# Split constant loads, early row ends, more fillers and a new list of steps in a state-space, MLP and expert kernel

## The chip, the cores and the metric

The kernel runs on one core of a Trainium2 chip, in one launch. The metric is the device time of that launch in microseconds (us). Five engines take part, each with its own stream of instructions: PE (matmuls, with its weight loads listed apart as PEld), DVE (vector), ACT (scalar), POOL (GpSimd) and SP (which here mostly issues DMAs). An engine runs its stream in order; where one needs what another makes, it waits on a semaphore.

## The reference, cut to what matters

```python
# stage 1: state-space recurrence; batch 4, heads 8, sequence 768, head size 32, state 16
log_a = np.log(np.clip(a, 1e-06, 1.0))
for c in range(768 // 32):
    cum = np.cumsum(la, axis=-1)                       # inside the chunk
    M = np.einsum('bhin,bhjn->bhij', Cc, Bc) * np.exp(cum_i - cum_j) * causal
    y = M @ xc + (Cc @ state) * np.exp(cum)
    state = np.exp(sum(la)) * state + sum_j Bc_j xc_j * np.exp(cum[-1] - cum_j)
x = y.transpose(0, 2, 1, 3).reshape(3072, 256)
# stage 2: dense MLP, d_ff 2048
x = np.maximum(x @ w_in, 0) ** 2 @ w_out
# stage 3: 8 experts, one for each token, d_ff 1024
logits = normalised(x) @ normalised(expert_emb).T / tau
e = argmax(logits); gate = softmax(logits)[e]
out = gate * (np.maximum(x @ w1[e], 0) @ w2[e])
```

## The kernel before, in words

The 3072 tokens are 24 tiles of 128 partitions, in 6 groups of 4. Stage 1 works a tile at a time: a few tables are made from the logarithms of the decays `a` by matmuls with constant masks (`tables` L1051, `tables2` L1065 and L1067, `tables3` L1084 and L1090; the masks are the constant `c1`, 128x903 in f32, of which columns 0 to 511 serve `tables`, columns 512 to 774 the two others, and 8 rows of the last 128 columns line L1090). Then come the scores (L811), their decay (DVE L829), the mask (POOL L837), the output (L922) and the state. The squares of each tile (ACT L949) decide its scale (DVE L968).

Stage 2 runs 16 blocks of d_ff for each group as "units" (first products L1250, relu and square on ACT and DVE, second products L1269); they fill PE from about 37 us to 343 us, beside stage 1 of later tiles. When a group is ready, `route` picks each token's expert and POOL scatters the rows to a table in DRAM, ordered by expert (L1461, an indirect DMA for each tile).

Stage 3 is 31 "jobs" of up to 128 rows of one expert: 13 from a first table made after group 4, 15 from a second, and 3 under an If. A job is: `job_load` (SP, transposed read of the rows, L1607), first products (L1634, 12 matmuls), relu in two parts (ACT L1714, DVE L1716), a transpose by DMA (SP L1645), second products (L1662 and L1664, 8 pairs), `job_result` (ACT L1677, then DVE L1680, both scaled by the gate), `job_send` (POOL L1687, indirect DMA to the output). The gate and the destination of a row stand in four 16-bit columns at its end, 512 to 515. `job_ends` reads these (a DMA on ACT's queue, L1703) and multiplies the gate by a factor on DVE (L1705). The numbers of rows and experts come into registers by `load_regs` (L1553), on PE once for each table.

The order of all this is written out by hand: each piece of work is a Python generator that yields its engine and an assumed duration (`yield "T", 2.6` is PE for 2.6 us), and `weave()` (L390) takes the next step of the generator that the table `ORDER` names. What it emits, the engines run in that order. The durations decide nothing of the order where the table names each step; they are used in one more place, `keep_warm` (L474): where the plan leaves PE idle in the beginning, it puts filler matmuls (L477, 128x176 on zeros, results unused), so many for each planned idle microsecond (4.799 up to 6 us, 4.8 later). The filler's zeros are written by DVE first (L1898).

SP's loads go through `load` (L483, issue at L485). The first ones are a part of C (`ct`), the decays, `c1`, the expert embedding, `b_t`, `tau` and two pieces of w_in, then `x`, `bc` (B and C by token) and `c2`.

Of the kernel before, what the change touches and what calls it, by code (L numbers as in the profile page):

```python
# [9 lines left out]
F32 = mybir.dt.float32  # L10
# [6 lines left out]
ALU = mybir.AluOpType  # L17
# [7 lines left out]
H = 8  # L25
# [27 lines left out]
           q1=343.921, q2=43.866, q3=196.988, slack=0.043, warm=4.8, cold=4.799, u0=0.5, d0=97.094, m0=24.87,  # L53
           m1=1.248, u1=17.747, du=77.015, t0=111.371, t1=50.866, t2=54.217, t3=156.529, t4=129.206, t5=39.718,
           oz=3.191, oa=57.9, ob=23.917, ou=158.402, oc=-54.916, og=172.157, ol=101.876, ev=-1.454, fin=10.03,
           rt=-25.056, fin5=77.015, rt5=83.245, e0=75.531, e1=19633888, e2=0.024, e3=2113488, wi=0.043, pi=48831578,
           pi1=-87.702, wo=61.294, po=0.263, po1=0.042, l1=69.922, emb=129.297, con=-28.03, fj=63.956, fe=92.693,
           oj=48519990, pd=95.005, oe=83.994, lj=-6.608, l0=199.952, v0=0.75, v1=0.25, v2=1, ps=176, wq=-6.586,
           c0=71.046, c1=-111.128, uh=43.261, mh=52.693, sn=14)

ORDER = (
# [1912 lines left out]
```

## Time and profile before

| | us |
|---|---|
| median of 3 runs | 510.75 (509.02 to 510.91) |
| the profiled execution's own time | 510.88 |
| its span in the trace | 509.2 |
| PE busy | 486.0 (95%) |
| ACT, DVE, POOL busy | 350.9, 321.2, 158.0 |

The span is that of the trace; 1.7 us of the execution's own time lie around it. PE busy 95% of the span means that only 23 us are left in which PE does nothing, 7.5 of them behind its last matmul. The share says nothing on where these are, nor which of the busy time is fillers. The clock granted to PE is 0.988 of the full one on average: it was full except between about 9 and 16 us, where it was half. The chain that ended last goes through PE for 70% of the span, DVE and DMA for 8% each and ACT for 6%.

### The profile page before, as it was taken

How to read it: one execution, taken by the hardware profiler on the slowest of the kernel's cores; microseconds unless marked ns; L12 is line 12 of the kernel's file. 1: busy time of each engine (PE TensorE's matmuls, PEld its weight loads, DVE VectorE, ACT ScalarE, POOL GpSimd, SP SyncE). 2: the span in 40 equal slices, each digit the busy share in tenths (PEclk: the TensorE clock that was granted, in tenths of full speed). 3: DMA queues.
4: the chain of work that ended last, by engine and by line, in shares of the span. 5: the costliest groups of instructions: out<-in, count | busy, mean ns of one | idle time of the engine just before them, and what ended most of it. 6: DMA issues, size and time to landing. Idle time of an engine off the chain costs nothing.

```text
span 509.2 us, 11796 instructions
## 1 busy us (share of the span) xinstructions
PE 486.0 (95%) x4057; PEld 316.8 (62%) x4057; DVE 321.2 (63%) x917; ACT 350.9 (69%) x735; POOL 158.0 (31%) x186
## 2 busy tenths in 40 slices
PE   8889999999999999999999999999998989999994
PEld 7656467766776776676667676665554445455552
DVE  4788966788868988868656856855764223234331
ACT  3889896698989889999999999875232123233321
POOL 0667655556574332500210120110030403031222
PEclk8899999999999999999999999999999999999997
DMA  8980003355153651335405231024898659797872
GB/s 280 404 313 2 2 11 106 105 157 164 41 201 54 156 136 44 115 115 187 176 33 121 98 127 31 23 66 81 137 197 158 165 117 177 124 182 142 142 127 58
DMA packets 112204, 64.59 MB, mean 127 GB/s; under 512 B 101253, under 2 KB 105615, under 8 KB 109072
## 3 DMA queue, kind: packets, MB, share of 16 engines
q1 hardware_dynamic: 105616, 57.38, 45.7%
q0 software_dynamic: 2496, 6.40, 3.7%
q10 hardware_dynamic: 4032, 0.03, 0.6%
q8 instruction: 36, 0.59, 0.5%
q14 instruction: 24, 0.20, 0.1%
HBM read 32.58 MB, written 8.13 MB: 80 GB/s over the span
## 4 chain that ended last, share of the span: by engine, by line
PE 70%; DVE 8%; DMA 8%; ACT 6%; issue 5%; ACTq 0%; POOL 0%; POOLq 0%; SPq 0%; DVEq 0%
PE bank L1250 20%; PE bank L1269 17%; PE bank L1634 10%; DMA out<-work 6%; PE bank L1662 5%; PE bank L811 3%; PE bank L922 2%; PE bank L1664 2%; PE bank L1159 2%; DMA work<-xs 1%; PE bank L917 1%; PE bank L1198 1%; ACT wexp L693 1%; PE bank L989 1%; DVE wexp L829 1%
## 5 line engine op out<-in xcount | busy, mean ns | idle before, releaser
L1250 PE MATMUL bank<-work 128*128 128x256 f16 x1152 | 136.5, 273 | 1.3 <-DVE work L1290 1.3
L1250 PEld LDWEIGHTS <-work 128*128 128x128 f16 x1152 | 111.4, 98 | 24.3 <-issue 2.0
L1269 PE MATMUL bank<-work 128*128 128x512 f16 x480 | 113.3, 379 | 0.0
L1662 PE MATMUL bank<-wexp,work 128*128 x224 | 74.0, 379 | 4.9 <-DVE work L1680 2.5
L1634 PE MATMUL bank<-wexp,work 128*128 x336 | 76.5, 379 | 1.1 <-DVE work L1716 1.1
L1269 PEld LDWEIGHTS <-work 128*128 128x128 f16 x480 | 46.3, 99 | 43.9
L1714 ACT ACTIVATE work<-bank 128x512 f16<-128x512 f32 x56 | 32.0, 597 | 54.4 <-PE bank L1634 36.7
L1461 POOL DMA_INDIRECT xs<-work x24 | 27.4, 1141 | 114.2 <-ACT work L1274 73.7
L1687 POOL DMA_INDIRECT out<-work x28 | 27.3, 975 | 112.6 <-DVE work L1680 70.8
L1664 PE MATMUL bank<-wexp,work 128*128 x224 | 61.0, 273 | 0.0
L1290 DVE TENSOR_TENSOR work<-work 128x512 f16<-128x512 f32 x68 | 46.2, 687 | 20.3 <-ACT work L1286 19.9
L1634 PEld LDWEIGHTS <-work 128*128 128x128 f16 x336 | 32.6, 98 | 37.9 <-issue 1.5
L837 POOL TENSOR_SCALAR_AFFINE_SELECT wexp<-wexp 128x512 f32<-128x512 f32 x48 | 36.4, 758 | 62.5 <-DVE wexp L829 45.4
L1716 DVE SCALAR_TENSOR_TENSOR work<-bank,work 128x512 f16<-128x512 f32 x56 | 36.8, 684 | 27.4 <-ACT work L1714 26.6
L1274 ACT ACTIVATE work<-bank 128x512 f32<-128x512 f32 x80 | 47.1, 591 | 10.0 <-PE bank L1269 7.4
L1286 ACT CAST work<-work 128x512 f16<-128x512 f32 x80 | 48.7, 616 | 3.1 <-DVE work L1282 2.0
L1677 ACT ACTIVATE work<-bank,work 128x256 f32<-128x256 f32 x28 | 13.2, 474 | 51.8 <-PE bank L1664 21.0
L829 DVE TENSOR_TENSOR wexp<-bank,wexp 128x256 f32<-128x256 f32 x96 | 37.9, 416 | 6.5 <-PE bank L811 4.5
L1279 ACT ACTIVATE work<-work 128x512 f32<-128x512 f32 x64 | 40.2, 630 | 0.4
L1662 PEld LDWEIGHTS <-work 128*128 128x128 f16 x224 | 21.9, 98 | 26.6 <-issue 0.5
L1680 DVE SCALAR_TENSOR_TENSOR work<-bank,work 128x256 f32<-128x256 f32 x28 | 13.5, 481 | 26.0 <-ACT work L1677 25.7
L1664 PEld LDWEIGHTS <-work 128*128 128x128 f16 x224 | 21.9, 98 | 9.5 <-issue 5.2
(246 smaller groups left out, 743.4 us busy)
## 6 DMA issues: line engine op xcount, KB each, us to landing
wexp<-in_w SPq DMA_DIRECT2D x8, 1024.0 KB
work<-in_w SPq DMA_DIRECT2D x8, 1024.0 KB
wexp<-in_w_in SPq DMA_DIRECT2D x4, 1024.0 KB
wexp<-in_w_out SPq DMA_DIRECT2D x4, 1024.0 KB
wexp<-in_x SPq DMA_DIRECT2D x6, 512.0 KB
wexp<-in_ct SPq DMA_DIRECT2D x6, 256.0 KB
wexp<-in_bc SPq DMA_DIRECT2D x6, 256.0 KB
xs<-work SPq DMA_DIRECT2D x9, 132.0 KB
```

The lines of the kernel that those rows point to most:

```text
L829: V.tensor_tensor(mv, ps.rearrange("p (a b) -> p a b", b=32), eg[:, t, n * q:n * q + n].rearrange("p h q -> p (h q)").unsqueeze(2) .to_bro ...
L837: G.affine_select(out=mm, in_=mm, pattern=[[0, 4], [1, P]], compare_op=ALU.is_ge, fill=0.0, base=0, channel_multiplier=-1)
L1250: T.matmul(po, gg[:, s], wout[:, wi, f], start=(f == 0 and n == 0 and k % 2 == 0), stop=(f == NF - 1 and n == 2), skip_group_check=True)
L1269: T.matmul(p, win[:, wi, kk, f * P:(f + 1) * P], x[:, xi * 2 + kk], start=(n == 0), stop=(n == 5))
L1274: S.activation(r, p, AF.Relu, scale=XK)
L1279: S.activation(r, r, AF.Square)
L1286: S.copy(gh, r)
L1290: V.tensor_tensor(gl, r, gh, ALU.subtract)
L1634: T.matmul(p, xj[i][:, xi * 2 + kk], W[:, bass.ds(e, 1), c0:c0 + 512].rearrange("p a b -> p (a b)"), start=(n == 0), stop=(n == 5))
L1662: T.matmul(po, r[:, f], W[:, bass.ds(e, 1), c0:c0 + 512].rearrange("p a b -> p (a b)"), start=(f == 0), stop=False, skip_group_check=True)
L1664: T.matmul(po[:, 0:DM], r[:, 8 + f], W[:, bass.ds(e, 1), c0:c0 + 256].rearrange("p a b -> p (a b)"), start=False, stop=(f == 7), skip_grou ...
L1716: V.scalar_tensor_tensor(out=rh[:, 1, s], in0=p, scalar=0.0, in1=rh[:, 0, s], op0=ALU.max, op1=ALU.subtract)
```

## The change

All arithmetic stays, apart from the number of fillers (55 before, 75 now). The changed parts are:

- `c1` is loaded in three pieces, first columns 512 to 774, then 0 to 511, then the 8 rows of 128, each with a mark of its own that the tables wait for.
- The decays are loaded by a DMA on ACT's queue, the first thing in ACT's stream, ahead of its table load; before, SP issued it second.
- The filler's zeros are written by POOL instead of DVE.
- `job_ends` starts with the job's row load instead of behind the transpose of its relu, and has 13 buffers for its factor instead of 5, so that it needs no result of the job two before.
- The last job (27) does its eight 512-wide second products first and the eight 256-wide ones behind them.
- Many assumed durations are new, the fillers are 6.5 (up to 7 us) and 11 (later) for each planned idle microsecond, and the table `ORDER` is new from end to end.

```diff
-           q1=343.921, q2=43.866, q3=196.988, slack=0.043, warm=4.8, cold=4.799, u0=0.5, d0=97.094, m0=24.87,
+           q1=343.921, q2=43.866, q3=196.988, slack=0.043, warm=11, cold=6.5, u0=0.5, d0=97.094, m0=24.87, m1=1.248,
...
-    "3.1 0 1 23 3.0 23.0 7 8 3.2 3.3 24 15 15 5 23 19 21 17 5 16 23 45 23 23 21 19 5 22 45 17 23 23 23 5 21 55 22 "
+    "0 1 5.1 3 5.0 2 4 6.0 5.3 5.2 9 10 6.1 26 17 17 7 24 24 18 47 7 7 47 19 23 19 7 23 57 69 20 21 22 23 21 8 57 "
...
-    ffj = [A.take([1], F32) for _ in range(5)]
+    fft = A.take([16], F32)
+    ffj = [fft[:, i:i + 1] for i in range(13)]
...
-                keep_warm((s - free[eng]) * (DUE["warm"] if s > 6 else DUE["cold"]))
+                keep_warm((s - (free[eng] or 0.5)) * (DUE["warm"] if s > 7 else DUE["cold"]))
             free[eng] = s + cost
-            th[2] = s + cost + LAT
+            th[2] = s + cost + LAT + sum(what for what in th[3][2:] if type(what) is float)
...
@@ job_load
         reads_rows(Q.dma_start_transpose(out=xj[i].bitcast(I16), in_=row_at(r, 0, 512)), table)
         yield "mark", ("xj", j)
+        yield "spawn", job_ends(j, table)
...
@@ job
         Q.dma_start_transpose(out=rT[j % 4], in_=flat(rh))
         yield "mark", ("rT", j)
-        yield "spawn", job_ends(j, table)
         yield "due", job_due(j)
...
-        yield "T", 2.6, (pbank(j),)
+        last = j == JU - 1
+        yield "T", 1.73 if last else 2.6, (pbank(j),)
         for f in range(8):
...
-            T.matmul(po[:, 0:DM], r[:, 8 + f], W[:, bass.ds(e, 1), c0:c0 + 256].rearrange("p a b -> p (a b)"),
-                     start=False, stop=(f == 7), skip_group_check=True)
+            if not last:
+                low_half(j, f)
+        if last:
+            yield "mark", ("m2h", j)
+            yield "T", 0.95, (pbank(j),)
+            for f in range(8):
+                low_half(j, f)
...
@@ job_ends
-        yield "need", ("rows_s", table)
-        yield "need", ("out", before(j, 2))
-        yield "need", ("sent", j - NXJ)
-        yield "S", 0.45
+        for key in (("rows_s", table), ("out", j - NXJ), ("sent", j - NXJ)):
+            yield "need", key
+        yield "S", 0.4, 4.2
         reads_rows(S.dma_start(fi[i].bitcast(I16), xs[bass.ds(rows_s[j], P), 512:516]), table)
         yield "V", 0.1, "L"
-        V.tensor_tensor(ffj[j % 5], fi[i][:, 0:2].bitcast(F32), fjob[:, j:j + 1], ALU.mult)
+        V.tensor_tensor(ffj[i], fi[i][:, 0:2].bitcast(F32), fjob[:, j:j + 1], ALU.mult)
...
-    th = [(0, load(flat(la), a_tok, 0.27, ("ald", 0))), (DUE["lc"], load(c1_s, c1, 2.3, ("c1", 0))),
+    k0 = 4 * P, 6 * P + 7
+    th = [(-1e3, log_inputs()), (DUE["lc"], load(c1_s[:, k0[0]:k0[1]], c1[:, k0[0]:k0[1]], 0.5, ("c1", 0))),
+          (DUE["lc"], load(rr_s, c1[0:H, k0[1]:], 0.05, ("c1", 2))), (DUE["lc"], load(c1_s[:, 0:k0[0]], c1[:, 0:k0[0]], 0.8, ("c1", 1))),
...
-        V.memset(idle_s, 0.0)
+        G.memset(idle_s, 0.0)
+        S.dma_start(flat(la), a_tok)
         S.preload_act_table_set("natural_log_exp_and_others")
-        free["S"] = 1.3
+        free.update(S=1.8, V=1.0, G=0.6, Q=0.8)
```

SP's loads now come in the order `c1` (128x263), `ct`, `c1` (128x512), `b_t`, `c1` (8x128), `c2`, `bc` twice, `x`, w_in twice, `ct`, w_in twice, the embedding and so on; `tau` is the 23rd load instead of the 6th. The embedding's preparation (L1099, some ten small instructions on DVE) stands among tiles further on.

The first place is PE's stream at the start. Before, 26 fillers stand ahead (the last is the first row here), then the tables (L1065, L1084, L1051), a sum over C (L755) and the first tile's scores (L811):

```order
L477 MATMUL bank_67<-wexp 128x176
L1065 MATMUL bank_69<-wexp 128x32
L1084 MATMUL bank_64<-wexp 8x5 x4
L1051 MATMUL bank_69<-wexp 128x32 x4
L755 MATMUL bank_63<-wexp 128x128 x4
L1084 MATMUL bank_64<-wexp 8x5 x20
L1090 MATMUL bank_64<-wexp 128x20
L811 MATMUL bank_67<-wexp 128x128
L811 MATMUL bank_68<-wexp 128x128
```

Now 22 fillers stand ahead (L478 is the old L477, L1089 the old L1084, L756 the old L755, L1056 the old L1051):

```order
L478 MATMUL bank_67<-wexp 128x176
L1089 MATMUL bank_64<-wexp 8x5 x20
L756 MATMUL bank_63<-wexp 128x128 x4
L1056 MATMUL bank_69<-wexp 128x32 x4
L1089 MATMUL bank_64<-wexp 8x5 x4
L478 LDWEIGHTS wexp
L478 MATMUL bank_67<-wexp 128x176
L478 LDWEIGHTS wexp
```

The table with the 128x263 piece comes first, the 128x32 matmul of L1065 has gone behind the first tile's scores (as L1070), and five fillers (two of them shown) stand ahead of the scores. The seven fillers that stood between the first and the second tile's scores are gone from there; seven now stand behind the second tile's scores and the first tile's output.

The second place is ACT's stream in the jobs. Before, loads of row ends (L1703) stand one by one among the relus (L1714) and the results (L1677):

```order
L1714 ACTIVATE work<-bank_68 128x512
L1714 ACTIVATE work<-bank_64 128x512
L1703 ISA
L1703 DMA work<-xs 128x4
L1714 ACTIVATE work<-bank_63 128x512
L1714 ACTIVATE work<-bank_67 128x512
L1703 ISA
L1703 DMA work<-xs 128x4
L1677 ACTIVATE work<-bank_65,work 128x256
L1703 ISA
L1703 DMA work<-xs 128x4
L1714 ACTIVATE work<-bank_68 128x512
```

Now (L1720 is the old L1703, L1731 the old L1714, L1695 the old L1677):

```order
L1731 ACTIVATE work<-bank_67 128x512
L1731 ACTIVATE work<-bank_68 128x512
L1720 ISA
L1720 DMA work<-xs 128x4
L1720 ISA
L1720 DMA work<-xs 128x4
L1437 ACTIVATE work<-work 128x32
L1720 ISA
L1720 DMA work<-xs 128x4
L1720 ISA
L1720 DMA work<-xs 128x4
L1720 ISA
```

All thirteen loads of the first table's row ends now stand ahead of the second job's result, and five of them directly behind one another but for one small instruction (L1437); before, two loads stood ahead of that result. The next loads follow when the second table is there.

The third place is POOL's stream, where the last group's scatters (L1461) stand among the sends (L1687). Before:

```order
L1461 DMA xs<-work 25728x528 x15
L1810 IOTA work 128x1
L1687 DMA out<-work 3072x256
L1461 DMA xs<-work 25728x528 x3
L1687 DMA out<-work 3072x256 x2
L1461 DMA xs<-work 25728x528
L1687 DMA out<-work 3072x256 x23
```

Now (L1467 and L1705 are the old L1461 and L1687):

```order
L1467 DMA xs<-work 25728x528 x12
L1827 IOTA work 128x1
L1705 DMA out<-work 3072x256 x2
L1467 DMA xs<-work 25728x528 x4
L1705 DMA out<-work 3072x256 x24
```

The four scatters of the last group stand together behind two sends; before, three stood behind one send and the fourth behind three. On PE, the register load for the second table's experts (L1553, now L1559) stood directly behind the first products of job 12 and ahead of the second products of job 8; it now stands behind the second products of jobs 7 and 8 and ahead of those of job 9.

## Rows read from the trace of the kernel before

**Rows 1.** Busy time by stretch: window, its length, busy us of each engine, clock, DMA.

```profile
core 0: us, PE busy (x) PEld busy (x) DVE busy (x) ACT busy (x) POOL busy (x), PEclk, DMA share, GB/s
0.00:37.00 37.00, 30.96 (x385) 24.33 (x385) 25.35 (x87) 24.58 (x47) 15.85 (x30) 0.91 0.90 334
10.00:15.00 5.00, 5.00 (x34) 4.38 (x34) 1.92 (x12) 2.54 (x8) 2.24 (x3) 0.50 1.03 386
15.00:20.00 5.00, 4.72 (x71) 3.74 (x72) 4.28 (x12) 4.16 (x9) 2.89 (x6) 0.91 1.05 412
37.00:343.00 306.00, 303.67 (x2813) 211.26 (x2814) 230.41 (x644) 277.78 (x588) 110.84 (x123) 1.00 0.33 95
343.00:380.00 37.00, 35.67 (x233) 19.72 (x231) 22.79 (x80) 14.55 (x36) 3.84 (x5) 1.00 0.75 130
380.00:502.00 122.00, 115.70 (x632) 61.52 (x629) 42.20 (x107) 33.71 (x66) 26.53 (x28) 1.00 0.79 148
```

**Rows 2.** Timeline of PE from 0 to 7 us: start, length, what.

```profile
1.15 3.99 PE L477 MATMUL bank<-wexp 128*128 128x176 f16 x26 [1.15 <-DVE wexp L1898]
6.16 0.38 PE L1065 MATMUL bank<-wexp 128*128 128x32 f32 x2 [1.02 <-DMA wexp<-in_c]
```

**Rows 3.** Chain of waits from 0 to 22 us: start, length, what.

```profile
1.76 4.26 DMA wexp<-in_c
...
7.83 0.97 PE bank L755 x8
8.80 1.08 PE bank L1084 x40
...
10.42 1.19 PE bank L811 x16
...
12.97 1.07 PE bank L1051 x4
14.04 1.03 PE bank L477 x7
15.06 1.05 PE bank L811 x16
...
18.04 0.81 PE bank L1051 x4
```

**Rows 4.** Timeline of SP, the load of the decays.

```profile
1.29 0.42 SPq L485 DMA_DIRECT2D wexp<-in_a  x1
```

**Rows 5.** Timeline of DVE, the clip of the decays.

```profile
4.00 0.26 DVE L1026 TENSOR_SCALAR wexp<-wexp 128x192 f32<-128x192 f32 x1 [2.49 <-DMA wexp<-in_a]
```

**Rows 6.** Timeline of POOL, the first product with B and C.

```profile
16.88 0.40 POOL L861 TENSOR_TENSOR wexp<-wexp 128x128 f32<-128x128 f32 x1 [2.13 <-DMA wexp<-in_bc]
```

**Rows 7.** What PE waited for from 343 to 503 us: total, times, longest.

```profile
PE bank L1662 <- DVE work L1680: 2.5, 2, 2.2
PE bank L1662 <- issue: 2.4, 1, 2.4
PE bank L1250 <- DVE work L1290: 1.3, 1, 1.3
PE bank L1634 <- DVE work L1716: 1.1, 1, 1.1
```

**Rows 8.** Chain of waits before the matmul at 388.22 us.

```profile
380.74 4.06 DMA work<-xs
```

**Rows 9.** Register loads of line 1553 on PE: durations ns, first and last start.

```profile
L1553 PEldq TENSOR_LOAD <-work x2: 1304/2378/3451, 343.5 to 405.3; - x2
```

**Rows 10.** Timeline of ACT, two loads of row ends in a row.

```profile
398.96 0.88 ACTq L1703 DMA_DIRECT2D work<-xs  x2
```

**Rows 11.** Timeline of POOL, the last group's fourth scatter.

```profile
398.83 0.97 POOL L1687 DMA_INDIRECT out<-work  x1 [17.33 <-DVE work L1531]
400.11 0.98 POOL L1461 DMA_INDIRECT xs<-work  x1 [0.30 <-issue]
```

**Rows 12.** Timeline of ACT, the last job's result.

```profile
501.79 0.47 ACT L1677 ACTIVATE work<-bank,work 128x256 f32<-128x256 f32 x1 [2.12 <-PE bank L1664]
```

More of the change, by code (lines that the diff above doesn't have):

```diff
@@ L52 @@
            g3=-57.34, dl=1, dl1=0, s0=1636976993, s1=0.5, s2=0.875, bs=1, qx=84.622, qb=89.036, qc=19.985, q0=89.631,
-           q1=343.921, q2=43.866, q3=196.988, slack=0.043, warm=4.8, cold=4.799, u0=0.5, d0=97.094, m0=24.87,
[L54 to L59, printed above, removed]
-ORDER = (
[87 rows of a table removed]
+           q1=343.921, q2=43.866, q3=196.988, slack=0.043, warm=11, cold=6.5, u0=0.5, d0=97.094, m0=24.87, m1=1.248,
+           u1=17.747, du=77.015, t0=111.371, t1=50.866, t2=54.217, t3=156.529, t4=129.206, t5=39.718, oz=3.191,
+           oa=57.9, ob=23.917, ou=158.402, oc=-54.916, og=172.157, ol=101.876, ev=-1.454, fin=10.03, rt=-25.056,
+           fin5=77.015, rt5=83.245, e0=75.531, e1=19633888, e2=0.024, e3=2113488, wi=0.043, pi=48831578, pi1=-87.702,
+           wo=61.294, po=0.263, po1=0.042, l1=69.922, emb=129.297, con=-28.03, fj=63.956, fe=92.693, oj=48519990,
+           pd=95.005, oe=83.994, lj=-6.608, l0=199.952, v0=0.75, v1=0.25, v2=1, ps=176, wq=-6.586, c0=71.046,
+           c1=-111.128, uh=43.261, mh=52.693, sn=14)
+ORDER = (
[87 rows of a table added]
 ).split()
@@ L564, in conv64 @@
         c = 3
-        yield "T", 0.32, (c,)
+        yield "T", 0.17, (c,)
         xb = x.bitcast(BF16).rearrange("p (e w) -> p e w", w=2)
@@ L613, in scale64 @@
         yield "need", ("c2", 0)
-        yield "T", 0.15, (c,)
+        yield "T", 0.25, (c,)
         T.transpose(row, m, ident_s)
@@ L617, in scale64 @@
         V.tensor_reduce(out=m[0:1], in_=row, op=ALU.max, axis=AX.X)
-        yield "T", 0.15, (c,)
+        yield "T", 0.33, (c,)
         T.matmul(bank[c][:, P:P + 1], onef_s[0:1, :], m[0:1], start=True, stop=True, skip_group_check=True)
@@ L691, in expert @@
         for b in range(nb):
-            yield "S", 2.1 / nb
+            yield "S", 1.9 if nb == 1 else 0.6
             S.activation(junk[:, b], blocks[:, b], AF.Square, accum_out=nn[:, b:b + 1])
@@ L783, in ssm_bt @@
         bp = bank[5][:, 320:448]
-        yield "T", 0.17, (5,)
+        yield "T", 0.12, (5,)
         T.transpose(bp, bg[g % 2][:, k], ident_s)
@@ L816, in ssm_b @@
         yield from scores_need(t)
-        yield "T", 0.7, tuple(bs)
+        yield "T", 0.95, tuple(bs)
         scores(t)
@@ L864, in ssm_u @@
         if t < NAPART:
-            yield "T", 0.27, (5,)
+            yield "T", 0.28, (5,)
             outer_products(t)
@@ L908, in ssm_c @@
                 yield from scores_need(t + 1)
-            yield "T", 1.6 if c else 1.35, (4, 5, 6, 7)
+            yield "T", 1.75 if c else 1.4, (4, 5, 6, 7)
             if t + 1 < NTILE:
@@ L952, in scaled_tile @@
             T.matmul(tbank[:, 0], one_b, sq[:, hf * P:hf * P + P], start=(hf == 0), stop=(hf == 1), skip_group_check=True)
-        yield "V", 0.35, (6, 7)
+        yield "V", 0.47, (6, 7)
         V.tensor_scalar(out=hb.bitcast(I32), in0=tbank[:, 0].bitcast(I32), scalar1=24, scalar2=23,
@@ L974, in scaled_tile @@
         yield "need", ("xs", t - 1)
-        yield "T", 0.15, (6, 7)
+        yield "T", 0.24, (6, 7)
         T.matmul(tbank[:, 1, 0:1], sb, ident_s[:, 0:1], start=True, stop=True, skip_group_check=True)
@@ L986, in ssm_d @@
             yield "need", key
-        yield "T", 0.24, (6, 7)
+        yield "T", 0.25, (6, 7)
         for hf in range(2):
@@ L1020, in ssm_d, with log_inputs @@
         yield "mark", ("d", t)
+    def log_inputs():
+        yield "S", 0.01, 1.2
+        yield "mark", ("ald", 0)
     def logs():
@@ L1043, in tables @@
         yield "need", ("la", 0)
-        yield "need", ("c1", 0)
+        yield "need", ("c1", 1)
         b = bank[7 if i == 0 else 1]
@@ L1048, in tables @@
             yield "need", ("egx", q - 2)
-            yield "T", 0.1 * m if i == 0 else 0.7, (7 if i == 0 else 1,)
+            yield "T", 0.23 * m if i == 0 else 0.8, (7 if i == 0 else 1,)
             for r in range(m):
@@ L1063, in tables2 @@
         b, o = (bank[7], P) if i == 0 else (bank[2], 0)
-        yield "T", 0.1 if i == 0 else 0.7, (7 if i == 0 else 2,)
+        yield "T", 0.31 if i == 0 else 1.1, (7 if i == 0 else 2,)
         T.matmul(b[:, o:o + n], wm_s[:, 5], lf, start=True, stop=True, skip_group_check=True)
@@ L1081, in tables3 @@
         o, o2 = (424, 448) if i == 0 else (320, 320)
-        yield "T", 0.055 * nt, (c,)
+        yield "T", 0.07 * nt if i == 0 else 1.08, (c,)
         for t in range(nt):
@@ L1088, in tables3 @@
         V.tensor_copy(tf, bank[c][0:H, o:o + 5 * nt])
+        yield "need", ("c1", 2)
         yield "T", 0.3, (c,)
@@ L1156, in unit0 @@
             yield "order", ("h%d" % h, f - 1)
-        yield "T", 0.86 * n + 0.1, (f % 2,)
+        yield "T", 0.87 * n + 0.06, (f % 2,)
         for kk in range(2):
@@ L1459, in route @@
         for k in range(4):
-            yield "G", 1.04, "R"
+            yield "G", 1.28, "R"
             wrote_rows(G.indirect_dma_start(
@@ L1670, in job, with low_half @@
                 yield from job_send(j)
+    def low_half(j, f):
+        c0 = 4096 + f * 512
+        T.matmul(bank[pbank(j)][:, 0:DM], rT[j % 4][:, 8 + f],
+                 W[:, bass.ds(es[j], 1), c0:c0 + 256].rearrange("p a b -> p (a b)"), start=False, stop=(f == 7),
+                 skip_group_check=True)
     def job_result(j):
-        ff = ffj[j % 5]
+        ff = ffj[j % NXJ]
         po = bank[pbank(j)]
@@ L1685, in job_send @@
         yield "need", ("out", j)
-        yield "G", 1.04, "R"
+        yield "G", 1.28, "R"
         sends_rows(G.indirect_dma_start(out=out, out_offset=bass.IndirectOffsetOnAxis(ap=fi[i][:, 2:4].bitcast(I32), axis=0),
@@ L1816, in pads @@
         for e in range(E):
-            yield "Q", 0.6, 0.3
+            yield "Q", 1.5, 0.3
             prs = load_regs(prow[0:1, e:e + 1], 1, SP, DUMMY)
```

172 rows, old and new, of the table ORDER are left out of this document.

## The prediction

> **What bounds the kernel now.** I read the busy time by stretch first. From 37 to 343 us PE is busy 303.67 of 306 us at full clock [rows 1]: the dense stage is PE's, and a new order can find at most 2.3 us there. From 343 to 380 us PE idles 1.33 us, from 380 to 502 us 6.30 us, so the jobs hold 7.63 us. Before 37 us it idles 37.00 - 30.96 = 6.04 us, and part of its busy time there is fillers. Behind PE's last matmul lie 7.5 us of result, send and landing, which the change leaves as they are. PE's real work is the same before and after, instruction for instruction; so the time can move only through idle time, fillers on the path and the clock.
>
> Then I read the two ends closely. At the start PE runs 26 fillers in 3.99 us (0.153 each), then waits 1.02 us for the constants, and does its first useful matmul at 6.16 us [rows 2]. The chain of waits leads back to the one load of 451.5 KB, 4.26 us from issue to landing, and from 6.16 us on it is PE itself up to the second tile's scores at 15.06 us, seven fillers (1.03 us) included [rows 3]. Within it the clock is half: 0.50 from 10 to 15 us [rows 1], so that two matmuls of L1051 take 1.07 us, and 0.81 us later at full clock [rows 3].
>
> In the jobs the list of waits names four causes, which add up to 7.3 us [rows 7]: second products behind a result on DVE (2.5), behind "issue" (2.4), a unit behind DVE L1290 (1.3) and first products behind the relu on DVE (1.1). The first is a chain: ACT's result waits for DVE L1705, this for a row-end load that was issued at 380.74 us and took 4.06 us [rows 8]. The "issue" is a register load on PE, 3.45 us against 1.30 us the first time [rows 9].
>
> **The change part by part.** The profiled execution took 510.88 us, 509.2 of them the span; the median is 510.75, so the sum may be made against 510.9.
>
> Start. The decays were issued at 1.29 us [rows 4] and their clip began at 4.00 us [rows 5], 2.7 us later. Issued at about 0.8 us by ACT they should be there at 3.5 us and their logarithm at about 4.1 us. The first piece of the constants is 263 of 903 columns and is issued first instead of third, 0.9 us earlier; I estimate its landing at 3.5 to 4 us. So the 22 fillers decide: from 1.15 us, 22 x 0.153 = 3.4, first useful matmul at 4.55 us instead of 6.16. POOL writes their zeros now; it is idle there, and half a microsecond more or less is in the range. Then in the new order: 20 small matmuls of L1084 1.08 (8.80 to 9.88), L755 0.97, that is 6.60 us against 8.80 before; L1051 about 1.0 and four small ones 0.28, 7.9; five fillers 0.77; scores at 8.66 us against 10.42: -1.76. Between the first and second tile's scores seven fillers go (-1.03), and come L785, L1065's 128x32, L1090 and L873, some 1.3 us. So the second tile's scores are still about 1.5 to 1.75 us early; I take -1.75. The half clock: had the chain run at full clock, L1051 would save 0.26, each set of scores some 0.1, the rest in like measure, about 1.2 us over the stretch. Whether denser fillers prevent it no row shows. Both ends are 0 and -1.2; I take half, -0.6.
>
> `bc` and `x` pass ahead of w_in, 2 x 1 MB earlier in the queue. POOL waited 2.13 us for `bc` [rows 6], and DVE idled 0.72 us between 15 and 20 us [rows 1]; I take half of that, -0.35, with ends 0 and -0.7. The embedding's preparation, some ten small DVE instructions of about 0.15 us, moves off DVE's idle early time to tiles behind the first ones, where DVE is busy 230 of 306 us [rows 1]; that cover hides it, and without it the cost would be 1.5 us. Start: -1.75 - 0.6 - 0.35 = -2.7, range -0.5 to -4.
>
> The gain depends on how much must land. The trace gives 4.26 us for the large piece and does not say which part is size and which is queueing. The Trainium skill ("DMA: Bandwidth & Descriptors", section "Issuing engines are not separate DMA queues") says that DMAs issued by different engines share the same 16 DMA engines, so that a second issuing engine saves only the time of the issue, which speaks against counting ACT's queue as a faster load. By it the decays come earlier by one issue slot alone, and the first matmul at about 5.0 us; the sum would be 0.4 us less.
>
> Middle. 2.3 us idle in 306 us. Nothing in the change aims there, but the table is new throughout, and an order worked out from planned durations can put a step in front of a late one; 0, with ends -1.5 and +1.5.
>
> Jobs. Row ends are loaded with the rows, so the load of 4.06 us is over long before the result. The wait of 2.2 us goes; what is late next at that place is the second part of the relu and its transpose, which had been done here when the result was not: -2.2. The register load stood directly behind job 12's first products, when the second table was just being made. It now has second products of jobs 7 and 8 ahead, and the fourth scatter of the last group, which waited behind a send that idled 17.33 us and came at 400.11 us [rows 11], comes with the other three. So the table is made earlier and PE asks later. I expect a plain load of 1.3 us as at first, which nothing hides: -1.2 of 2.4. Of the other 2.4 us (1.3 a register load at the first table as well as the wait named, 1.1 a relu) I take -0.4. Jobs: -3.8, ends 0 and -6.
>
> Thirteen loads on ACT come earlier, several in a row. One costs ACT about 0.44 us (two in a row took 0.88 us, [rows 10]), and ACT is busy 14.55 of 37 us from 343 to 380 us [rows 1]; so 13 x 0.44 = 5.7 us fit into the idle time. What waits behind them on ACT are relus, and behind these SP's transposes and PE's second products.
>
> Last job. Its result on ACT starts 0.1 us behind the last matmul and takes 0.47 us [rows 12]; to start it on the high half while PE does the low half could save up to 0.5. In the built kernel ACT's result waits for the last of the 16 matmuls as before. So 0, with ends 0 and -0.5. The Trainium skill ("PSUM — Partial Sum Buffer", section "PSUM bank collisions raise a hardware error") asks that PSUM be guarded by bank and quadrant and not by address, which speaks against the edit's aim: both halves are one bank. By it the gain is 0 as well; by the aim alone the sum would be 0.5 more. No run here shows a collision.
>
> Sum: -2.7 + 0 - 3.8 + 0 = -6.5; 510.9 - 6.5 = 504.4 us.
>
> **The rivals.** First, the start comes and the jobs only in part: the late row ends are replaced by SP's transpose of the relu as the last to come. For it: ACT's relus sit among long waits, and SP has a row load and a transpose for each job. Against it: PE waits for none of SP's in the list [rows 7]. The 2.2 us stays: 504.4 + 2.2 = 506.6.
>
> Second, the jobs come and the start doesn't: the first tiles are bound by DVE later anyway, or POOL's zeros and the clock eat the gain. For it: DVE is as busy as PE behind 20 us; against it: the chain up to 16 us is PE alone [rows 3]. 504.4 + 2.7 = 507.1.
>
> Third, neither: the new order swaps old waits for new ones of the same size all along, 510.5. The profile has nothing for it but that a plan is not a measurement.
>
> Fourth, slower: the row of loads blocks ACT. If each load has to wait for an earlier one to land, the five that follow one another take 5 x 4.06 = 20.3 us instead of 2.2, and relus, transposes and second products behind them come as late. PE has other jobs' first products for a while: a job takes 159 us / 28 = 5.7 us of PE. So it decides once the five take longer than one job, 5.7 us; at 20.3 us PE loses 14.6, and the time is 504.4 + 14.6 = 519 us. Against it stands the row of two loads issued within 0.88 us, the second before the first can have landed [rows 10]. For it, that no row shows more than two.
>
> **How the numbers follow.** What a measurement of this kernel can tell from no change is about 0.5%, 2.55 us: faster is below 508.2. Forecast (both terms, 504.4, its own range 501 to 507): 0.56. First rival 0.14, second 0.13, third 0.10, fourth 0.07. Faster: 0.56 + 0.13 + 0.11, a little of the first two being near the bound, 0.80. Same 0.12: the third and what was taken off. Slower 0.08, the fourth and a little of the middle's +1.5 with the third. The range goes from 500.0 (start -4, jobs -6, middle -0.9) to 508.6, which takes in the first two rivals and leaves out the fourth and most of the third.
>
> **What would show it.** Start: first useful matmul at 4.3 to 4.9 us with no wait for the constants, first scores before 9 us, tile squares (L949) 2 us earlier. Clock: the row from 10 to 15 us above 0.50, or not. Jobs: no wait of ACT's result for DVE L1705, second products with no wait over 1 us on a result, PE's register load at 1.3 us. End: the result on ACT still starts behind the last matmul. The prediction is wrong if PE's idle time from 343 to 502 us stays above 6 us, if a row of loads on ACT takes 4 us each, or if the middle loses more than 1.5 us.

## The result, and the profile after

The changed kernel takes 504.72 us (median of 4 runs, 502.85 to 507.04), the kernel before 510.41 (4 runs): ratio 0.988, 95% interval 0.9844 to 0.9915. The prediction was 504.4. The total is right; three of its four terms are not, and the rest of this document is about that. Seven further executions of the changed kernel on another occasion (e7) took 502.92 to 513.36 us, median 510.50, against 510.99 for the kernel before on the same chip, so that four near 504.4 are in part luck. Ratios here leave out executions that were slower than the fastest of their kernel by over 1.5% (four of e7's seven and five of e4's twelve, the profiled ones among them); medians hold all.

The busy time by stretch of the kernel after, to be laid beside [rows 1] (same columns; four windows are new):

```profile
core 0: us, PE busy (x) PEld busy (x) DVE busy (x) ACT busy (x) POOL busy (x), PEclk, DMA share, GB/s
0.00:37.00 37.00, 30.41 (x408) 24.26 (x409) 27.18 (x80) 24.87 (x47) 18.61 (x32) 0.98 0.85 327
32.00:36.00 4.00, 1.14 (x5) 0.55 (x4) 3.90 (x12) 2.64 (x6) 1.45 (x3) 0.95 0.38 144
36.00:40.00 4.00, 4.00 (x15) 2.78 (x18) 1.83 (x8) 1.58 (x4) 3.62 (x4) 0.62 0.00 0
37.00:343.00 306.00, 305.61 (x2839) 213.83 (x2838) 235.40 (x654) 277.63 (x587) 106.64 (x124) 1.00 0.35 97
343.00:380.00 37.00, 36.54 (x230) 19.46 (x229) 23.89 (x92) 15.02 (x37) 1.97 (x2) 1.00 0.75 133
380.00:497.00 117.00, 112.62 (x606) 59.51 (x603) 39.02 (x91) 33.05 (x64) 28.20 (x29) 0.99 0.84 151
407.00:411.00 4.00, 4.00 (x17) 2.01 (x15) 0.00 (x0) 0.00 (x0) 0.00 (x0) 0.59 0.50 96
```

PE's idle time before 37 us has not fallen (6.59 us, 6.04 before). In the dense middle it fell from 2.33 to 0.39 us, from 343 to 380 us from 1.33 to 0.46. Behind that 4.38 us are left of 6.30, nearly in one piece, as the lists of what PE waited for show (total, times, longest; 0 to 37 us, then 330 to 503 us):

```profile
PE bank L616 <- DVE work L611: 1.8, 1, 1.8
PE bank L478 <- POOL wexp L1917: 1.2, 1, 1.2
PE bank L1165 <- DVE work L960: 1.1, 1, 1.1
...
PE bank L1669 <- issue: 4.1, 1, 4.1
PE bank L1641 <- DVE work L1733: 0.5, 1, 0.5
```

Of the four waits in [rows 7] the 2.5 us behind a result and both others are gone or halved; the "issue", 2.4 us before, is 4.1 now. It is the register load again: [rows 9] had 3451 ns for the second one, now

```profile
L1559 PEldq TENSOR_LOAD <-work x2: 1306/2732/4157, 336.8 to 402.3; - x2
```

Idle time and time lost to the clock don't tell where the two kernels stand at one moment, since the order of work differs. So I count equal work: each matmul counts with the median of its duration over all traces of this study, fillers (the idle-time matmuls of `keep_warm`) with nothing (444 us in all). Mark A is where 40 us of such work are done (67 us on the clock), mark B where 290 us are (340 us). The spells are stretches at the 1.2 GHz level before 60 us that follow a first one at full clock, and "first rise" is where the first record of the full clock begins.

| kernel, profiled execution | to A | A to B | B to PE's end | first rise | spells | median us | ratio to before |
|---|---|---|---|---|---|---|---|
| before | 67.3 | 272.3 | 162.2 | 5.6 | 6.8 | 510.4 | |
| before again | 73.4 | 272.2 | 160.4 | 16.3 | 13.7 | | |
| after | 67.4 | 268.6 | 160.8 | 4.9 | 3.4 | 504.7 | 0.988 |
| after again (e7) | 71.6 | 268.6 | 161.2 | 4.0 | 17.1 | 510.5 | 0.986 (0.979 to 0.993) |
| e1 casts moved | 67.8 | 268.6 | 160.7 | 13.8 | 3.4 | 505.8 | 0.983 (0.978 to 0.988) |
| e2 register load 9 us earlier | 74.1 | 268.6 | 157.3 | 13.1 | 13.7 | 508.3 | 0.987 (0.982 to 0.992) |
| e3 row ends late | 71.7 | 268.6 | 162.6 | 4.2 | 17.1 | 511.3 | 0.988 (0.982 to 0.994) |
| e4 old filler rule | 75.2 | 269.3 | 161.8 | 4.1 | 30.7 | 513.4 | 0.992 (0.989 to 0.996) |
| e5 before, row ends early | 73.7 | 271.6 | 156.7 | 16.7 | 13.7 | 509.8 | 0.998 (0.994 to 1.001) |
| e8 loads of before | 75.0 | 268.4 | 159.8 | 4.1 | 20.5 | 515.3 | 1.010 (1.006 to 1.014) |
| e9 register load behind job 12 | 74.2 | 268.6 | 156.4 | 13.2 | 13.7 | 507.7 | 0.984 (0.978 to 0.990) |
| e6 both steps moved | 64.0 | 268.6 | 155.5 | 5.4 | 0.0 | 499.5 | 0.979 (0.974 to 0.984) |
| e6 again (e11) | 65.3 | 268.6 | 156.8 | 5.4 | 3.4 | 500.9 | 0.974 (0.970 to 0.979) |

From A to B the changed order takes 268.6 us in eight executions (268.4 and 269.3 in e8 and e4), the order before 272.3 and 272.2 in two. To A one kernel differs by 1 to 6 us from one execution to the next, with the spells.

Variants of one kernel can be compared in this way. The two kernels can not, since scores and output products are short in most records and long in some: from the start of one to the start of the next the median is 0.007 us, the mean 0.03 to 0.04. A tile that falls on the other side of a mark is so counted with too little, and between the marks the kernel before works a tile more (busy time by line, 68 to 339 us before, then 68 to 335 us after):

```profile
L811 PE MATMUL bank<-wexp 32*128 32x128 f32 x256 | 12.0, 296 | 0.0
L812 PE MATMUL bank<-wexp 32*128 32x128 f32 x240 | 10.9, 296 | 0.0
```

Two places need no weights. Ahead of the first job's first matmul (L1634, now L1641) both kernels have done exactly the same matmuls, fillers aside. Ahead of the sixth tile's scores (L811, now L812) they have too, but for some 0.7 us that the changed kernel still owes. PE's timelines, two rows before and two after:

```profile
40.65 0.73 PE L811 MATMUL bank<-wexp 32*128 32x128 f32 x16
347.42 7.93 PE L1634 MATMUL bank<-wexp,work 128*128 x36
39.79 0.73 PE L812 MATMUL bank<-wexp 32*128 32x128 f32 x16
342.56 4.05 PE L1641 MATMUL bank<-wexp,work 128*128 x18
```

By these marks the changed kernel is 0.9 us ahead at the sixth tile, gains 4.0 us from there to the first job (306.77 us, now 302.77; 306.72 in the second trace of before) and 0.1 us from there to PE's end (154.28, now 154.21; 152.51 in the second trace of before). Of the 4.0 us 3.3 are idle time of PE (3.66, now 0.39), 1.3 of them the wait for DVE L1290 of [rows 7]; 0.7 are busy time.

### The profile page after: what moved, and what is told of

It reads as the page before. It is cut to its first block, busy times and chain, and to the rows that moved or that the text cites. A ratio compares the mean times of both kernels' runs of the same rounds, so it can differ in the third digit from the quotient of the medians.

```text
span 504.2 us, 11884 instructions
## 1 busy us (share of the span) xinstructions
PE 485.2 (96%) x4077; PEld 317.1 (63%) x4077; DVE 326.0 (65%) x916; ACT 350.9 (70%) x735; POOL 156.4 (31%) x187
## 4 chain that ended last, share of the span: by engine, by line
PE 73%; issue 7%; DMA 7%; ACT 5%; DVE 5%; POOL 1%; SPq 1%; POOLq 0%; ACTq 0%; DVEq 0%
PE bank L1256 23%; PE bank L1275 18%; PE bank L1641 10%; PE bank L1669 5%; DMA out<-work 4%; PE bank L1165 3%; PE bank L1686 3%; PE bank L812 2%; PE bank L1204 2%; PE bank L923 2%; DMA wexp<-in_w_in 2%; PE bank L918 1%; DMA work<-xs 1%; POOL out L1705 1%; PE bank L990 1%
## 5 line engine op out<-in xcount | busy, mean ns | idle before, releaser
L1641 PE MATMUL bank<-wexp,work 128*128 x336 | 76.3, 379 | 0.5 <-DVE work L1733 0.5
L1731 ACT ACTIVATE work<-bank 128x512 f16<-128x512 f32 x56 | 32.3, 595 | 56.6 <-PE bank L1641 41.7
L1705 POOL DMA_INDIRECT out<-work x28 | 27.2, 973 | 125.6 <-DVE work L1698 74.6
L1467 POOL DMA_INDIRECT xs<-work x24 | 27.1, 1128 | 103.8 <-ACT work L1292 39.6
L1296 DVE TENSOR_TENSOR work<-work 128x512 f16<-128x512 f32 x68 | 47.4, 706 | 16.3 <-ACT work L1292 16.0
L1641 PEld LDWEIGHTS <-work 128*128 128x128 f16 x336 | 32.7, 98 | 37.6 <-issue 1.2
L838 POOL TENSOR_SCALAR_AFFINE_SELECT wexp<-wexp 128x512 f32<-128x512 f32 x48 | 33.7, 702 | 55.3 <-DVE wexp L830 36.7
L1695 ACT ACTIVATE work<-bank,work 128x256 f32<-128x256 f32 x28 | 13.0, 472 | 48.0 <-PE bank L1686 30.4
```

What stands on the lines that cost most here:

```text
L838: G.affine_select(out=mm, in_=mm, pattern=[[0, 4], [1, P]], compare_op=ALU.is_ge, fill=0.0, base=0, channel_multiplier=-1)
L1296: V.tensor_tensor(gl, r, gh, ALU.subtract)
L1641: T.matmul(p, xj[i][:, xi * 2 + kk], W[:, bass.ds(e, 1), c0:c0 + 512].rearrange("p a b -> p (a b)"), start=(n == 0), stop=(n == 5))
```

## The experiments

**e1: five small DVE instructions moved** (the constants: two casts, two tensor_scalars, a copy). Where PE waits at 32 to 36 us, DVE is full. Timelines of POOL and DVE after, and in the last row of DVE before (start, length):

```profile
29.36 2.40 POOL L584 TENSOR_TENSOR work<-work,wexp 128x1024 f32<-128x1024 f32 x1 [0.44 <-ACT wexp L582]
...
29.39 2.41 DVE L1778 CAST work<-work 128x18 f32<-128x18 int32 x1
...
33.52 0.68 DVE L611 TENSOR_REDUCE work<-bank 128x1 f32<-128x512 f32 x1
...
26.78 0.17 DVE L1761 CAST work<-work 128x18 f32<-128x18 int32 x1
```

A cast of 18 columns takes 2.41 us and ends when POOL's instruction does. Before, it ran with POOL idle and took 0.17.

```diff
 61   (DVE L884, at 18.2 us)
+26   (constants: DVE L1778 to L1782)
 ...
 34   (PE L567)
-26   (constants)
```

> The changed kernel with one step elsewhere: the five small DVE instructions of constants (L1778 to L1782) stand 58 steps earlier, at about 18.5 us, where POOL's long tensor_tensor (L584, 2.40 us) does not run. In the changed kernel L1778 took 2.41 us (0.17 before) while L584 ran beside it, in a stretch from 26 to 35.5 us in which DVE was never idle. Theory: DVE is held while POOL's instruction reads its operands, and DVE's stretch sets when the dense units start. Then L1778 takes 0.2 us, the units' first long run (L1165 at 35.62 us) starts at 33 to 34 us, and the time falls by 1.5 to 4 us, the larger figure if the half-clock spell of 3.4 us that followed PE's waits there goes too. Rival: the start of the units is bound by the conversion of w_in on ACT and its load. Then L1165 still starts at 35 to 36 us and the time is the same within 0.5 us.

The long hold is gone (L1778 took 0.17 us, the longest of the five 0.90). Yet L1165's long run, the one of eight, started at 37.85 us, not at 33 to 34: this execution's clock rose at 13.8 us only, 9 us later than in the changed kernel's trace, and a spell began at 34.3. Against e2 and e9, where it rose as late (13.1 and 13.2 us) and the casts stood where they were, it is 0.7 us earlier. PE in the changed kernel, in e1 and in e2:

```profile
35.62 3.68 PE L1165 MATMUL bank<-work,wexp 128*128 128x256 f32 x8 [1.08 <-DVE work L960]
37.85 1.89 PE L1165 MATMUL bank<-work,wexp 128*128 128x256 f32 x8
38.54 3.78 PE L1165 MATMUL bank<-work,wexp 128*128 128x256 f32 x8 [0.98 <-DVE work L960]
```

Where the clock rises early the theory's size comes: 33.9 us in e6 and 34.7 in e11 (a spell from 32.7 us), both with the casts moved, against 35.6 to 35.7 in the changed kernel, e7 and e3. So the hold is shown, and at this point it is worth 0.7 to 1.7 us. The total shows little of it (0.983).

**e2: PE's register load 9 us earlier.**

```diff
 341  (PE, second half of job 11's first products)
+316  (PE, register load for the second table)
 343  (PE, job 12's first products)
 ...
 335  (PE, job 8's second products)
-316
```

> The changed kernel with PE's register load for the second table moved ahead of the first products of job 12, about 9 us earlier; the table is ready there (its last cast ends at 388.7 us, the load came at 402.3 us and took 4.16 us, in which PE did nothing for 4.14 us). Theory: the load of 18 registers takes 1.5 us when the DMA engines are quiet and is stretched when they are full (1.48 us at a DMA share of 0.00, 1.59 at 0.23, 1.68 at 0.39, 3.21 at 0.93, 3.45 at 0.94, 4.16 at 1.03). At the new place the share is about 0.2 to 0.6, so the load takes 1.5 to 2.2 us, PE idles under 2 us there, no half-clock spell follows, and the time falls by 2.5 to 4 us. Rival: PE's load of this table costs 3.4 to 4.2 us wherever it stands, because PE has to run empty first. Then the gap stays above 3 us and the time is the same within 1 us.

The load took 2.87 us, PE idled 1.19 us beside it, no spell followed, and B to the end shrank by 3.5 us. (PE idled another 0.93 us 4.5 us ahead of the load, behind "issue"; e1, e3, e9 and e11 have such a wait of 1.0 to 1.8 us, in one piece or several, between 387 and 398 us, wherever the load stands; e6, e7 and the changed kernel's first trace have none. Its cause stays open.) The theory's place and price hold, its reason only in part: the load was not as short as said. The total (0.987) does not show it; this execution had spells of 13.7 us at its start, which the edit doesn't touch.

**e3: row ends late in the new order.**

```diff
 job_load(j)
-  job_ends(j): DMA on ACT, product on DVE
 job_result(j - 2)
+  job_ends(j): DMA on ACT
 ...
+  job_ends(j): product on DVE
 job_result(j)
```

> The changed kernel with the early row ends undone: each load of row ends (L1720) stands behind the result of the job two before, and its product on DVE directly ahead of the job's own result, for 27 of 28 jobs, as in the kernel before. PE's order is the same. Theory: the early row ends are worth the 2.2 us that PE waited before; with them late PE waits 2 us or more for results again, DVE and ACT wait for the landing (about 4 us) several times, and the time rises by 2 to 5 us. Rival: the new order of the jobs covers the landing, PE waits under 0.5 us more, and the time is the same within 1 us.

B to the end rose by 1.4 to 1.8 us. The total (0.988) does not show it. DVE waited for landings again, 14.7 us in 9 waits, and PE idled in five new places of 0.36 to 1.47 us. Two of these (1.47 and 0.36) are the "issue" wait named under e2; the three others, 1.7 us, are what the late row ends cost in this trace. DVE's waits from 343 to 505 us:

```profile
DVE work L1722 <- DMA work<-xs: 14.7, 9, 6.6
```

**e4: the old filler rule** (40 fillers instead of 75).

```diff
-warm=11, cold=6.5
+warm=4.8, cold=4.799
-keep_warm((s - (free[eng] or 0.5)) * (DUE["warm"] if s > 7 else DUE["cold"]))
+keep_warm((s - free[eng]) * (DUE["warm"] if s > 6 else DUE["cold"]))
```

> The changed kernel with the old rule for fillers (4.799 for each planned idle microsecond up to 6 us, then 4.8, counted from 0): 40 fillers instead of 75. Theory: the denser fillers keep the clock at full up to 35 us; with few of them half-clock spells come back before 30 us, the first tiles run later, and yet the time changes by less than 1 us, since DVE bounds the stretch from 26 to 35 us. Rival one: the clock stays full without them, since PE no longer waits for the constants; then nothing before 30 us changes but the fillers' own time and the time is the same. Rival two: the lost clock goes straight through to the end, +2 to +3 us.

The clock fell at 7.5 us for 13.7 us, as it did in the kernel before at 9 us for 6.8. Busy time by stretch of e4 (columns as above):

```profile
5.00:10.00 5.00, 4.75 (x63) 3.97 (x60) 1.65 (x6) 1.60 (x3) 0.71 (x1) 0.75 1.04 353
10.00:15.00 5.00, 5.00 (x39) 4.24 (x37) 1.80 (x12) 1.45 (x6) 2.26 (x4) 0.50 1.02 421
15.00:20.00 5.00, 5.00 (x46) 3.66 (x46) 3.28 (x11) 2.65 (x7) 2.79 (x8) 0.50 1.02 423
```

L1165's long run started at 39.4 us instead of 35.6. So the lost clock is not absorbed by DVE's bound; the second rival is nearer. The fillers are worth 3.8 us at that point, three times the far end that the prediction gave for the clock (1.2 us). In the total it is 0.992 against 0.983 to 0.988 for e1 to e3 on the same chip, with intervals that overlap.

**e5: early row ends alone, in the kernel before.**

```diff
 job_load
+        yield "spawn", job_ends(j, table)
 job
-        yield "spawn", job_ends(j, table)
 ORDER: job_ends(j) on ACT behind job_ends(j - 3)'s old place; PE's order kept
```

> The kernel before with the early row ends alone: the loads of row ends (L1703) stand three jobs earlier on ACT, with 13 buffers, their products on DVE where they were. PE's order is that of before. Theory: in the old order too the late row ends cost PE the 2.2 us wait; it goes, PE's jobs (from 347 us to its last matmul, 154.1 us before) take 1.5 to 2.5 us less, and the time falls as much. Rival: the relu's transpose is as late as the row ends were; the wait gets another name and the jobs take the same within 0.7 us.

B to the end fell by 3.7 to 5.5 us (against the two traces of before), more than the theory said. PE's waits from 343 to 505 us, against four in [rows 7]:

```profile
PE bank L1251 <- DVE work L1291: 1.3, 1, 1.3
PE bank L1663 <- DVE work L1681: 1.0, 1, 1.0
```

The "issue" is gone with the 2.2 us, though the register load still took 3.51 us and stood where it had stood. With job 12's first products not held up, PE had 3.7 us of them in hand when the load began; so part of this gain is the register load's. In the total (0.998) it does not show; this execution's start had 13.7 us of spells, which the edit doesn't touch, and that the other runs had as many was not traced.

**e6, e9 and e11: the register load directly behind job 12's first products** (all), and the casts of e1 (e6 and e11).

```diff
 343  (PE, job 12's first products)
+316  (PE, register load for the second table)
 333  (PE, job 7's second products)
 335  (PE, job 8's second products)
-316
```

> The changed kernel with two steps moved: the small DVE casts to 18.5 us as in e1_cast_moved, and PE's register load directly behind job 12's first products, ahead of the second products of jobs 7 and 8 (some 5 us earlier than in the changed kernel), where the DMA engines moved nothing for 2 us in the changed kernel's trace. Theory (the load is stretched by full DMA engines): it takes 1.4 to 1.8 us there, PE's gap is 1.2 to 1.8 us, less than the 2.1 us that the two gaps of e2_reg_early had, and PE's jobs are about 3 to 4 us shorter than in the changed kernel run beside it. Rival (a load of 18 registers costs PE 2.3 us or more at any place): gap 2.3 us or more, jobs at most 2 us shorter.

> The changed kernel with PE's register load for the second table directly behind job 12's first products, and nothing else: the first half of e6_both. Theory: the load's price is its own length (2.3 to 4.4 us in the profiles so far) less the work that PE has in hand when it starts (0.2 us behind second products, 2.9 and 3.7 us behind first products); here the load takes 3 to 3.5 us and the gap is under 0.7 us, PE's jobs are 5 to 6 us shorter than in the changed kernel, as in e6_both, while the start (DVE held by POOL for 2.4 us, units at 35.6 us or later) and its half-clock spells stay. Rival: the gain in the jobs of e6_both hung on its earlier start; then the gap is above 2 us here.

> The version with both steps moved (e6_both) a second time. Theory: without the 2.4 us for which POOL holds DVE the dense units start at 33.9 us where the clock rises early, and without PE's long waits at 32 to 36 us and at the register load fewer half-clock spells follow: 497 to 502 us where the changed kernel takes 503 to 513, ratio to before 0.975 to 0.985. Rival: e6_both met a quiet chip by chance; then a spell of 10 us or more at the start is found here and the ratio is 0.985 or more.

In e6 the load took 3.22 us and the gap was 0.48. First its load, then PE's timeline around it:

```profile
L1559 PEldq TENSOR_LOAD <-work x2: 1314/2264/3215, 333.4 to 391.0; - x2
```

```profile
388.80 5.13 PE L1641 MATMUL bank<-wexp,work 128*128 x23
394.41 0.38 PE L1669 MATMUL bank<-wexp,work 128*128 x1 [0.48 <-issue]
```

The load began at 391.0 us, PE worked until 393.93. In the changed kernel it began at 402.31 us and PE's work in hand ended at 402.53. In e9 and e11 the load took 1.70 and 1.63 us and PE idled nowhere beside it. B to the end is 155.5 to 156.8 us in all three, 4 to 6 less than in the changed kernel. e11's 1.3 us more than e6 are the "issue" wait named under e2 (1.68 us). e6's own theory was wrong on the length, and the gain was larger than it said; e9's price, length less work in hand, holds for every trace, with 0.2 us more (the eight here and the five others):

| kernel | length us | in hand us | gap us | DMA share during the load |
|---|---|---|---|---|
| before | 3.45 | 1.24 | 2.42 | 0.94 |
| after | 4.16 | 0.22 | 4.14 | 1.03 |
| after again | 3.87 | 0.20 | 3.87 | 1.07 |
| e4 | 4.37 | 0.22 | 4.36 | 1.12 |
| e1 | 2.34 | 0.22 | 2.33 | 0.76 |
| e5 | 3.51 | 3.70 | none | 1.20 |
| e6 | 3.22 | 2.94 | 0.48 | 0.90 |
| e9 | 1.70 | all of it | none | 0.25 |

With the casts moved as well the units' long run starts at 33.9 us in e6, not 35.6. The casts of e6, then its PE (DVE and PE timelines):

```profile
18.54 0.17 DVE L1778 CAST work<-work 128x18 f32<-128x18 int32 x1
```

```profile
33.91 1.99 PE L1165 MATMUL bank<-work,wexp 128*128 128x256 f32 x8 [0.35 <-DVE work L960]
```

No spell followed in e6, one of 3.4 us in e11. Ratio 0.979 and 0.974: this version beats both kernels, the changed one too (its highest of 12 runs, 502.7 us, is below the lowest of that kernel's 11, 502.85 us, though not all ran on one chip; on the chip that both shared it is 497.09 to 501.96 against 502.92 to 513.36).

**e7 and e10: each kernel once more.**

> The changed kernel, unchanged, on the same chip as its variants. Theory: what differs between executions of one kernel lies in the first 70 us and in the register load: PE's pace from 67 to 340 us repeats within 0.1 us, the first 70 us vary by several us with the half-clock spells. Then the time from equal work at 67 us to equal work at 340 us is 268.5 us again (272.1 in the kernel before). Rival: the middle's gain of 3.6 us was chance too, and this trace has 270 us or more.

> The kernel before, unchanged, for a second trace of it. Theory: from equal work at 67 us to equal work at 340 us it takes 272.2 us again, its jobs 161 us with the 2.2 us wait for a result and the 2.4 us register load; only the first 70 us differ, by the half-clock spells. Rival: its middle or its jobs vary by more than 1 us from one execution to the next, and the differences found by these sections are chance.

The middle repeats, 268.6 and 272.2 us. In the changed kernel again a cast was held, the next of the five this time (timelines of POOL and DVE):

```profile
29.43 2.44 POOL L584 TENSOR_TENSOR work<-work,wexp 128x1024 f32<-128x1024 f32 x1 [0.46 <-ACT wexp L582]
...
29.52 2.38 DVE L1779 CAST work<-work 128x8 f32<-128x8 int32 x1
```

So it was in e2, e3, e4 and e8 (2.38 us each) and in e9 (2.41). In the kernel before the jobs took 160.4 us this time, 1.8 less, and the two waits that the prediction priced were half as long (PE's waits from 343 to 508 us, against 2.5 and 2.4 in [rows 7]):

```profile
PE bank L1662 <- DVE work L1680: 1.3, 1, 1.3
PE bank L1662 <- issue: 1.1, 1, 1.1
```

The load took 3.67 us, and PE had 2.8 us in hand, not 1.2. So for the jobs e10's rival holds: they vary by more than 1 us between executions of one kernel.

**e8: the loads of before in the new order.**

```diff
-Q: c1[:, 512:775]; ct; c1[:, 0:512]; b_t; c1[0:8, 775:]
+Q: ct; a; c1 (all 903 columns); b_t
-S.dma_start(flat(la), a_tok)
```

> The changed kernel with the loads at the start undone: the C part first, then the decays, then all 903 columns of the constants in one load, all on SP; the list of steps and the denser fillers stay (two more fillers). Theory: PE's first useful matmul moves from 4.6 to 6.0 us or later and the first tiles with it, but the start of the dense units (35.6 us) moves by less than 0.7 us, since DVE and the conversion of w_in bound it; the time is the same within 1 us where the clock is the same. Rival: the 1.5 us goes straight through, the units start at 37 us or later and the time rises by 1.5 us.

The rival is right and too small. PE waited as before and the clock fell at 7.5 us for 6.8 us, in spite of 77 fillers; the units' long run started at 39.8 us, 4.2 us later. The median rose by 4.8 us, 0.9%, against the changed kernel on the same chip (515.29, 510.50; the ratios of the table, 1.010 and 0.986, say more). What the decays' queue, the split and the order of the loads do one by one was not tried. PE's timeline of e8:

```profile
6.16 1.14 PE L1100 MATMUL bank<-wexp 128*8 128x5 f32 x40 [1.59 <-DMA wexp<-in_c]
7.23 1.85 PE L756 MATMUL bank<-wexp 128*128 128x128 f32 x8
```

## Why the prediction came out as it did

**The start (-2.7 said; -0.9 between the profiled pair at the sixth tile's scores, with some 0.7 us of work still owed).** Step by step it was right up to 30 us in the profiled execution. First useful matmul 4.55 us said (5.0 where the decays gain one issue slot alone), 4.53 measured; scores 8.66 said, 8.28 measured (start, length):

```profile
1.19 3.41 PE L478 MATMUL bank<-wexp 128*128 128x176 f16 x22 [1.19 <-POOL wexp L1917]
4.53 1.15 PE L1089 MATMUL bank<-wexp 128*8 128x5 f32 x40
...
8.28 0.80 PE L812 MATMUL bank<-wexp 32*128 32x128 f32 x16
```

The squares of the first tile came 4.2 us earlier (12.7 us, 16.9 before), and no spell came before 35 us, where the prediction took half of that gain. The fifth tile's scores began 3.3 us earlier (27.6 us, 30.9 before). Luck has a part in this: in e2 and e9, whose start is the same, the clock rose at 13 us and the first scores came at 10.30 us. The step that failed is the last of that part, that what is gained at the front is still there at the units: the early chain ran into DVE, which was held 2.4 us by POOL's tensor_tensor (start of PE's long run 35.6 us, 33.9 in e6 without it, 37.2 before); PE was busy 1.14 of 4 us, and the units then ran 3.4 us at half clock. The second rival named DVE and had 0.13. Before had no such hold, as there POOL was idle beside these casts: a step of the new order that stands well by planned durations and badly beside its neighbour. The Trainium skill ("SBUF — State Buffer", section "Who interferes with whom") says that DVE's casts, copies and tensor_scalar can need the port pair that GpSimd uses, and that whoever issues first keeps it for its whole instruction. This case's traces agree: a cast of 0.17 us took 2.38 to 2.41 us in the seven traces in which it stood beside POOL's long instruction, and 0.17 in the three in which it had been moved. Against e8 the new loads are worth more than -2.7 (4.2 us at the long run), since they also keep the clock: a wait of 1.59 us for the constants is followed by a spell there.

**The middle (0 said, ends of 1.5; -2.7 measured, the largest term).** That is the 4.0 us up to the first job less the 1.3 of the wait for DVE L1290, which the prediction has among the jobs. Wrong: I took the idle time of 2.33 us as all that an order could find and expected none of it, and the new order found 1.94. The other 0.7 us come from PE's busy time: from 37 to 343 us the same 304 scores (L811) and 40 transposes (L989) are busy 0.4 us less each than before, at the same clock. That the reason is which matmuls stand beside them was not tried, nor which step of the new list ended which wait.

**The jobs (-3.8 said; -1.4 against the first trace, 0.3 more against the second).** Nearly all of the 1.4 is the wait for DVE L1290 ahead of the first job. PE's idle time from 343 us on fell by 2.8 us in all, and 3.4 us at half clock cost some 1.7 of that again (an estimate, half the spell). The row ends were right in kind and too small: -3.7 to -5.5 alone (e5, with its part of the register load's gap), for -2.2, which itself was one execution's figure (1.3 in e10). Rival four, a blocked ACT, did not come: five loads left within 3.1 us (ACT's timeline),

```profile
364.46 0.34 ACTq L1720 DMA_DIRECT2D work<-xs  x1
364.68 0.59 ACT L1731 ACTIVATE work<-bank 128x512 f16<-128x512 f32 x1
364.97 0.34 ACTq L1720 DMA_DIRECT2D work<-xs  x1
365.15 0.60 ACT L1731 ACTIVATE work<-bank 128x512 f16<-128x512 f32 x1
365.52 1.02 ACTq L1720 DMA_DIRECT2D work<-xs  x1
365.63 0.24 ACT L1437 ACTIVATE work<-work 128x32 f32<-128x32 f32 x1
366.71 0.85 ACTq L1720 DMA_DIRECT2D work<-xs  x2
```

The register load is the step that failed. I took it for late because its table was late, and expected -1.2, with a length of 1.3 us as at the first table. But that load has 13 registers and this one 18, which took 1.63 us at the least (e11). It is +1.7, and a spell of 3.4 us behind it: the table had been ready since 388.8 us, the load came at 402.3, behind second products, where PE has nothing in hand. Here the new order gave away most of what the early row ends had brought.

**The last job (0).** Right: ACT's result starts 0.1 us behind the last matmul, as in [rows 12].

```profile
496.85 0.47 ACT L1695 ACTIVATE work<-bank,work 128x256 f32<-128x256 f32 x1 [2.17 <-PEq L1924]
```

So the sum was near by luck: -2.7 in the middle stood in for most of what the start (1.8) and the jobs (2.4) lost, and the four executions lay in the lower part of what this kernel's executions have.

## What to carry to other kernels

A term is safe only when the next engine on the way has been priced too: an early start is worth what is left of it where the engines meet again. A blocking register load costs its length less the work that its engine has in hand, so it belongs behind a run of work that waits for nothing. When one kernel's runs differ by more than the change is worth, compare stretches at equal work; a stretch that repeats within 0.1 us decides what the total can't. Take as marks places ahead of which both kernels have done the same instructions; where work must be weighted, a median is a bad weight for durations that are short in most records and long in some.

## What the runs showed of the hardware

The length of the same 18-register load goes with how full the DMA engines are: 1.63 and 1.70 us at shares of 0.21 and 0.25, 2.3 at 0.70 to 0.76, 3.2 to 4.4 at 0.90 to 1.20 (2.87 at 1.30 is the exception). That one makes the other was not tried by itself.

The clock's first rise comes at 4 to 5.6 us in eight of the thirteen traces and at 13 to 17 us in five, both in the same kernel (5.6 and 16.3 us before; 4.9 after and 13.1 in e2, whose start is the same). Ahead of it fillers follow one another by 0.147 us, as they do in the spells, behind it by 0.08. So the kernel before was at half clock not only from 9 to 16 us but up to 5.6 us as well, and the 26 fillers of [rows 2] ran at that pace. Later spells of 3.4 to 17.1 us began close behind stretches with PE waits (the first of the changed kernel, at 35.6 us, behind waits of 1.8 and 1.1 us). What sets their length stays open. One kernel's executions differ by up to 10 us (e7), twice the change; the two traces of the changed kernel, 4.6 us apart, have spells of 3.4 and 17.1 us.
